# The first chunks' work and weight conversions in another order, and a decay table per chunk, in a retention and two-layer-pair kernel

## The chip, the cores and the metric

The kernel runs on one core of a Trainium2 chip. Its time is device microseconds (us) of one execution, from runs that repeat the same kernel. The core has TensorE (PE: matmuls; PEld: its weight loads), VectorE (DVE), ScalarE (ACT), GpSimd (POOL) and SyncE (SP), which issues the DMAs here. Each engine takes its instructions strictly in the order of its own queue, and engines wait for each other through semaphores.

## The reference

Retention over 4 sequences of 576 tokens with 8 heads of 64, and behind it two feed-forward pairs with 2304 tokens, 512 channels and 2048 hidden channels, all in fp32:

```python
# q, k, v: (4, 8, 576, 64)
scores = np.matmul(q, k.transpose(0, 1, 3, 2)) / np.sqrt(64)
gamma = 1.0 - 2.0 ** (-5.0 - np.arange(8))
Dmat = np.where(rel >= 0, gamma[:, None, None] ** rel, 0.0)   # rel = query position - key position
x = np.matmul(scores * Dmat, v)            # -> (2304, 512), tokens by channels
h = np.maximum(x @ w1_in, 0.0)
x = (h * h) @ w1_out                       # first pair
h = x @ w2_in
out = (h * np.clip(h + 3, 0, 6) / 6) @ w2_out   # second pair
```

## The kernel before

Tokens lie in 18 chunks of 128. The first pair runs over five blocks of tokens (512, 384, 512, 384, 512), and within a block over 16 steps f of 128 hidden channels each. In a step `h_part` makes the hidden rows (12 matmuls into a bank `h`), a relu, a product and a cast make `g`, and `a_part` adds 12 matmuls into four accumulators `acc`. On TensorE the order is h(0), h(1), acc(0), h(2), acc(1), h(3), acc(2) and so on.

fp32 numbers are carried as two fp32r parts, a high one (a cast) and a low one (what the cast left over), and each product takes three matmuls: high by high, high by low, low by high. The weights come as 64-bit words and are made fp32 on the core: `scale_w` (two instructions on ScalarE, lines 143 and 144), `narrow_w` (two on VectorE, 161 and 162), `cast_w` (the high part, ScalarE, 170) and `low_w` (the low part, GpSimd or VectorE, 177). Each step has two such halves of 512 columns: (f, 0) for `h_part`, (f, 1) for `a_part`. All of this is done while block 0 runs, a few steps ahead of use.

Before the first step, block 0's own input must be made: retention of chunks 0 to 3, the functions `first_...`. For a chunk c: `first_scores` (16 matmul records into `sc`), `first_mask` (VectorE, two instructions, `p`), `first_v` (v times a power of the decay, in place in `kv`), `first_values` (`p` by v into `o`), `first_read` (the state of the chunks before by q, added into the same `o`; chunk 0 has none), `first_states` (k by v, summed over the chunks into `total`, which is half of the PSUM tile `sums0`), `first_copy` (`total` into `states` in SBUF for the next chunk's read), `first_scale` (`o` times the decay table, `xf`), `first_x` (high part of x, ScalarE) and `first_low` (low part of x). Chunk 0's output is the other half of `sums0`. h(0) is done in two halves of 256 tokens: chunks 0 and 1, then chunks 2 and 3.

The order of every engine's queue is the order in which these calls are written; nothing is moved by a scheduler (`tc.manual_schedule()`). The DMAs of the start go through one queue in the written order too. `idle_matmuls` are matmuls on zeros whose output nobody reads.

Of the kernel before, what the change touches and what calls it, by code (L numbers as in the profile page):

```python
# [11 lines left out]
F32 = mybir.dt.float32  # L12
# [77 lines left out]
def retention_moe_kernel(ctx: ExitStack, tc, qk, kv, w1, w2, cst, out):  # L90
# [114 lines left out]
    def load_t(c):  # L205
        if c:
            tag = (None, f"w{NF - 5}_0", f"w{NF - 2}_0", f"w{NF - 2}_1")[c]
            t = whi.tile([P, 2, NPAIR, P], F32, tag=tag, name=f"q_{c}")
        else:
            t = apool.tile([P, 2, NPAIR, P], F32, tag="q", name=f"q_{c}")  # L210
        nc.sync.dma_start(t, qk[c].rearrange("p x (n t) -> p x n t", n=NPAIR))
        ch[c] = [t[:, 0], t[:, 1]]
# [33 lines left out]
    def first_v(c, eng):  # L246
        v3 = ch[c][3].rearrange("p (h d) -> p h d", h=H)
        eng.tensor_tensor(v3, v3, vds[c].unsqueeze(2).to_broadcast([P, H, D]), ALU.mult)  # L248
# [11 lines left out]
                r = slice(64 * e, 64 * e + 64)  # L260
                nc.tensor.matmul(sc[:, e, p, :], kt[r, p, :], q[r, p, :], start=True, stop=True)

    def first_mask(c):
        sc = points.pop(c)
        t = whi.tile([P, 2, NPAIR, P], F32, tag=f"w{NF - 4}_{1 - c % 2}", name=f"p_{c}")

        mask = causal.unsqueeze(1).to_broadcast([P, NPAIR, P])
        for i in range(2):
            a, b = (x[:, :, 2 * i : 2 * i + 2] for x in (t, sc))
            nc.vector.tensor_tensor(a, b, mask.rearrange("p (e n) t -> p e n t", e=2), ALU.mult)  # L270
        probs[c] = t

    def first_out(c):
        if c == 0:
            outs[c] = sums0[:, 1].rearrange("p (n t) -> p n t", n=NPAIR)
        else:
            outs[c] = ps_h.tile([P, NPAIR, P], F32, tag="h", name=f"o_{c}")

    def out_matmuls(c, first, last, stationary, moving):
        for p in range(NPAIR):  # L280
# [15 lines left out]
    def first_read(c, first=False, last=False):  # L296
# [4 lines left out]
            c, first, last, lambda p, e: s[:, p, 64 * e : 64 * e + 64], lambda p, e: q[:, p, :]  # L301
        )

    def first_scale(c):
        x = xf[c] = whi.tile(
            [P, NPAIR, P], F32, tag=(f"w{NF - 7}_{c % 2}", f"w{NF - 8}_{c % 2}")[c // 2], name=f"xf_{c}"
        )
        if c == 0:
            nc.vector.tensor_tensor(x, outs[c], qd3, ALU.mult)
            return  # L310
        for p in range(NPAIR):
            nc.vector.scalar_tensor_tensor(
                x[:, p], outs[c][:, p], gcs[c][:, p : p + 1], qd3[:, p], ALU.mult, ALU.mult
            )

    def first_x(c):
        x = xs[0, 0][:, :, :, c * P : (c + 1) * P]
# [295 lines left out]
    def h_part(ph, blk, f, between=lambda: None):  # L613
        nb = BLOCKS[blk][0]
        w = wts[ph, f, 0]
        x = xs[ph, blk]
        hp = ps_h.tile([P, 512], F32, tag="h", name=f"h_{ph}_{blk}_{f}")
        def order(last):
            return [(c, wi, xi) for wi, xi in ((0, 0), last[::-1], last) for c in range(NC)]

        parts = 2 if ph == blk == f == 0 else 1
        for i in range(parts):
            ts = slice(i * nb // parts, (i + 1) * nb // parts)
            for k, (c, wi, xi) in enumerate(order((1, 0) if blk == 0 and i == 0 else (0, 1))):
                nc.tensor.matmul(  # L625
                    hp[:, ts],
                    w[:, wi, c * P : (c + 1) * P],
                    x[:, xi, c, ts],
                    start=k == 0,
                    stop=k == 3 * NC - 1,  # L630
                )
        r = tmpp.tile([P, 512], F32, tag="tmp", name=f"r_{ph}_{blk}_{f}")
        r = r[:, :nb]
        nc.scalar.activation(r, hp[:, :nb], AF.Relu)  # L634
        between()
        nc.vector.tensor_tensor(r, r, hp[:, :nb], ALU.mult)  # L636
# [212 lines left out]
    def idle_matmuls(n):  # L849

        t = ps_h.tile([P, 512], F32, tag="h", name="unread")
        for _ in range(n):
            nc.tensor.matmul(t[:, :P], nought, nought, start=True, stop=True)

    idle_matmuls(6)
    for t in state:
        nc.vector.memset(t, 0.0)
    nc.vector.memset(con3, 3.0)
    load_t(0)
    nc.sync.dma_start(con0[:, :QD0], cst[:, :QD0])  # L860
    load_t(1)
    load_kv(0)
    load_kv(1)
    load_w(0, 0, (0,))
    load_t(2)
    nc.sync.dma_start(con0[:, QD0:], cst[:, QD0:DK0])
    load_kv(2)
    load_t(3)
    load_kv(3)
    load_w(0, 1, (0,))  # L870
    load_w(0, 0, (1,))
    load_w(0, 1, (1,))
    for f in range(2, 4):
        load_w(0, f)
    nc.sync.dma_start(con, cst[:, DK0:])
    new_x(0, 0)

    first_scores(0)
    first_mask(0)
    first_scores(1)  # L880
    idle_matmuls(3)
    first_v(0, nc.vector)
    first_mask(1)
    first_states(0)
    first_v(1, nc.gpsimd)
    first_values(0, first=True, last=True)
    first_copy(0, act=False)
    first_values(1, first=True)
    scale_w(0, 0, (0,))
    first_read(1, last=True)  # L890
    narrow_w(0, 0, (0,))
    first_states(1)
    first_scores(2)
    first_copy(1, act=True)
    first_scale(1)
    first_v(2, nc.gpsimd)
    first_read(2, first=True)
    first_scale(0)
    first_x(1)
    first_mask(2)  # L900
    first_low(1, nc.gpsimd)
    first_x(0)
    first_states(2)
    cast_w(0, 0, (0,))
    first_scores(3)
    first_copy(2, act=True)
    low_w(0, 0, (0,))
    first_v(3, nc.vector)
    first_values(2, last=True)
    first_mask(3)  # L910
    first_read(3, first=True)
    first_low(0, nc.gpsimd)
    scale_w(0, 1, (0,))
    first_scale(2)
    first_states(3)
    first_values(3, last=True)
    first_scale(3)
    first_x(3)
    narrow_w(0, 1, (0,))
    first_x(2)  # L920
    first_low(3, nc.gpsimd)
    first_low(2, nc.vector)
    scale_w(0, 0, (1,))
    cast_w(0, 1, (0,))
    low_w(0, 1, (0,))
    scale_w(0, 2, (0,))
# [45 lines left out]
    def first_between(f):  # L972
        if f == 0:
            scale_w(0, 1, (1,))
        if f + 2 < NF:
            cast_w(0, f + 2, (0,))
            low_w(0, f + 2, (0,))

    for i, (ph, blk, f) in enumerate(steps):
        if blk == 0:  # L980
            if 1 < f:
                low_w(0, f, (1,), nc.vector)
            if f:
                scale_ahead(f, True)
            if 0 < f < NF - 2:
                narrow_w(0, f + 2, (0,))
            if 0 < f < NF - 1:
                narrow_w(0, f + 1, (1,))

        late = i >= len(steps) - 2  # L990
        if not late:
            unit_work(i - NF + 2, 0)
        if i + 1 < len(steps):
            h_part(*steps[i + 1], lambda: first_between(f) if blk == 0 else None)
            if i == 0:
                narrow_w(0, 1, (1,))
            if blk == 0 and f + 1 < NF:
                cast_w(0, f + 1, (1,))
            if i == 0:
                g_low(*steps[1])  # L1000
                low_w(0, 1, (1,), nc.vector)
                scale_w(0, 3, (0,))
                first_sum()
                scale_w(0, 2, (1,))
            if blk == 0 and f:
                scale_ahead(f, False)
        if blk == 0:
# [298 lines left out]
```

## Time and profile before

| | us |
|---|---|
| median of 3 runs | 802.19 (802.16 to 804.36) |
| the profiled execution | 803.26 |
| its span, first to last instruction | 801.5 |
| TensorE busy | 795.2 (99%) |
| VectorE, ScalarE, GpSimd busy | 592.3, 399.6, 165.3 |

The profile is of one execution, whose own time stands beside its span; the rest of its time lies around the span. A page of it has the busy time of each engine, the chain of work that ended last, and the costliest lines. Here 96% of that chain is TensorE. The timeline of an engine lists its instructions by start time; consecutive instructions of one line are merged with their count. "[0.63 <-DMA q]" at the end of a row is idle time of the engine before that row and what ended it.

### The profile page before, as it was taken

The numbers are of one execution on the slowest core, as the hardware profiler recorded it, in microseconds if no ns is written. First come the engines' busy times: TensorE is split into PE (matmuls) and PEld (weight loads), VectorE is DVE, ScalarE is ACT, GpSimd is POOL, SyncE is SP. The second block draws the span as 40 slices with busy tenths as digits, with TensorE's granted clock in tenths as the row PEclk, the third lists the DMA queues.
The fourth block names the chain that finished last, engine by engine and source line by source line (L and its number), as shares of the span: only waits on it lengthen the run. The fifth ranks groups of instructions, "written<-read, shape, count | busy, mean of one in ns | idle before, by whom it ended". The sixth has DMA issues, their size and how long they took to land.

```text
span 801.5 us, 16527 instructions
## 1 busy us (share of the span) xinstructions
PE 795.2 (99%) x6390; PEld 741.2 (92%) x6390; DVE 592.3 (74%) x1091; ACT 399.6 (50%) x741; POOL 165.3 (21%) x154
## 2 busy tenths in 40 slices
PE   9999999999999999999999999999999999999998
PEld 8788889999888899998888899999999999999998
DVE  5988987878755587776557866987577987677864
ACT  3797744444443444444435533666234655244553
POOL 3312230211011011100000065600255500256200
PEclk9999999999999999999999999999999999999999
DMA  9966637777756487856448888888887989878884
GB/s 345 344 201 237 220 93 210 220 224 223 221 149 188 125 257 213 232 159 186 143 133 267 248 300 254 306 302 298 273 264 245 350 260 304 277 244 264 265 277 144
DMA packets 148062, 189.66 MB, mean 237 GB/s; under 512 B 22416, under 2 KB 101904, under 8 KB 147984
## 3 DMA queue, kind: packets, MB, share of 16 engines
q1 hardware_dynamic: 147984, 188.61, 74.0%
q8 instruction: 50, 0.82, 0.5%
q14 instruction: 28, 0.23, 0.1%
HBM read 149.78 MB, written 38.80 MB: 235 GB/s over the span
## 4 chain that ended last, share of the span: by engine, by line
PE 96%; DMA 2%; POOL 1%; issue 1%; DVE 0%; POOLq 0%
PE acc L662 25%; PE h L625 24%; PE z L1196 22%; PE z L1251 21%; PE at L498 2%; DMA kv<-kv_dram 1%; POOL x L322 1%; POOL w L177 1%; PE alone L498 0%; DMA q<-qk_dram 0%; PE sc L410 0%; PE o L461 0%; PE sc L421 0%; PE o L471 0%; POOL kv L248 0%
## 5 line engine op out<-in xcount | busy, mean ns | idle before, releaser
L662 PE MATMUL acc<-g,w 128*128 128x512 f32 (+1 forms) x960 | 213.1, 370 | 0.3 <-POOL w L177 0.3
L625 PE MATMUL h<-x,w 128*128 128x512 f32 (+2 forms) x972 | 210.9, 365 | 1.3 <-ACT x L318 0.6
L625 PEld LDWEIGHTS h<-x,w 128*128 128x128 f32 x972 | 175.9, 188 | 24.0 <-ACT x L318 0.8
L662 PEld LDWEIGHTS acc<-g,w 128*128 128x128 f32 x960 | 173.8, 188 | 24.5 <-POOL w L177 0.6
L1196 PE MATMUL z<-xop,ring 128*128 128x384 f32 x1008 | 175.3, 334 | 0.0
L1196 PEld LDWEIGHTS z<-xop,ring 128*128 128x128 f32 x1008 | 174.7, 188 | 0.1
L1251 PE MATMUL z<-ring,spl 128*128 128x256 f32 x1512 | 172.2, 276 | 0.0
L1251 PEld LDWEIGHTS z<-ring,spl 128*128 128x128 f32 x1512 | 172.1, 188 | 0.0
L1112 POOL TENSOR_TENSOR aop<-aop,aop 128x384 f32<-128x384 f32 x96 | 106.6, 1122 | 293.4 <-DVE aop L1109 289.7
L1134 DVE TENSOR_TENSOR spl<-aop,spl 128x384 fp32r<-128x384 f32 x168 | 99.1, 608 | 30.6 <-ACT spl L1130 27.0
L1130 ACT ACTIVATE spl<-aop 128x384 fp32r<-128x384 f32 x168 | 86.4, 524 | 54.4 <-PE z L1251 49.6
L634 ACT ACTIVATE r<-h 128x512 f32<-128x512 f32 (+1 forms) x80 | 44.3, 554 | 109.7 <-PE h L625 109.6
L1106 ACT ACTIVATE aop<-held,small 128x384 f32<-128x384 f32 x72 | 44.5, 619 | 108.3 <-DVE held L1072 107.8
L636 DVE TENSOR_TENSOR r<-r,h 128x512 f32<-128x512 f32 (+1 forms) x80 | 50.6, 632 | 53.3 <-ACT r L634 52.8
L1072 DVE TENSOR_TENSOR held<-z,held 128x384 f32<-128x384 f32 x120 | 66.5, 554 | 28.5 <-PE z L1196 26.4
L638 ACT ACTIVATE g<-r 128x512 fp32r<-128x512 f32 (+1 forms) x80 | 47.3, 591 | 65.8 <-DVE r L636 65.8
L644 DVE TENSOR_TENSOR g<-r,g 128x512 fp32r<-128x512 f32 (+1 forms) x80 | 53.1, 663 | 20.9 <-ACT g L638 18.6
L1109 DVE SCALAR_TENSOR_TENSOR aop<-aop,held 128x384 f32<-128x384 f32 x72 | 50.2, 698 | 17.8 <-ACT aop L1106 16.2
L395 POOL TENSOR_TENSOR qs<-qs,con 128x512 f32<-128x512 f32 x11 | 15.6, 1416 | 138.5 <-DMA qs<-qk_dram 138.5
L752 ACT ACTIVATE uhi<-seven 128x896 fp32r<-128x896 f32 x32 | 30.6, 956 | 24.3 <-DVE seven L742 14.1
L757 DVE TENSOR_TENSOR seven<-seven,uhi 128x896 fp32r<-128x896 f32 x32 | 34.9, 1091 | 7.6 <-ACT uhi L752 7.2
L177 POOL TENSOR_TENSOR w<-wt,w 128x512 fp32r<-128x512 f32 x17 | 23.1, 1359 | 63.6 <-ACT w L170 57.0
(109 smaller groups left out, 611.9 us busy)
## 6 DMA issues: line engine op xcount, KB each, us to landing
ring<-w_out_hl SPq DMA_DIRECT2D x84, 512.0 KB, 5.0
ring<-w_in_hl SPq DMA_DIRECT2D x72, 512.0 KB, 4.6
raw<-w_dram SPq DMA_DIRECT2D x32, 512.0 KB, 7.0
uraw<-w_dram SPq DMA_DIRECT2D x64, 256.0 KB, 3.4
q<-qk_dram SPq DMA_DIRECT2D x18, 512.0 KB, 5.2
w_in_hl<-uhi SPq DMA_DIRECT2D x16, 448.0 KB, 3.8
w_in_hl<-seven SPq DMA_DIRECT2D x16, 448.0 KB, 4.7
w_out_hl<-uhi SPq DMA_DIRECT2D x16, 448.0 KB, 3.2
```

The costliest lines, as they stand in the source:

```text
L625: nc.tensor.matmul(hp[:, ts], w[:, wi, c * P : (c + 1) * P], x[:, xi, c, ts], start=k == 0, stop=k == 3 * NC - 1,)
L636: nc.vector.tensor_tensor(r, r, hp[:, :nb], ALU.mult)
L638: nc.scalar.activation(g[:, 0, :nb], r, AF.Copy)
L644: nc.vector.tensor_tensor(g[:, 1, :nb], r, g[:, 0, :nb].bitcast(F32), ALU.subtract)
L662: nc.tensor.matmul(acc[d][:, :nb], wt, g[:, gi, :nb], start=first, stop=stop)
L1072: fn(*a)
L1109: stt(f32(q, j), f32(q, j), 6.0, h, ALU.min, ALU.mult)
L1112: nc.gpsimd.tensor_tensor(f32(o, j), f32(a, j), f32(b, j), op)
L1130: act(t[:, 0, :], f32(q, k), AF.Copy)
L1134: tt(t[:, 1, :], f32(q, k), t[:, 0, :].bitcast(F32), ALU.subtract)
L1196: nc.tensor.matmul(bank[q], w[:, wi, u * P : (u + 1) * P], x[:, u, xi, :], start=k == 0 and q not in (2, 4, 3), stop=k == 5, skip_group_ch ...
L1251: nc.tensor.matmul(o, sp[:, g, P * n : P * (n + 1)], w[:, k % 2, wi, :], start=k == 0 and m == 0 and n % 2 == 0 and q not in (2, 4, 3), st ...
```

## The change

Seven things are changed, all ahead of step 2 of block 0:

- k and v of chunk 0 are loaded third, the decay table (`con0`, second part) fourth, w(0,0) of step 0 after k, v of chunk 2; among the later weights some change places.
- The idle matmuls are 7 and 5 in place of 6 and 3, and the 5 stand behind the scores of chunk 0.
- `first_scores` of a chunk stands behind `first_states` of the chunk before, not a chunk ahead; `first_read` stands ahead of `first_values`.
- `first_mask` may be called in two halves; `first_low` of chunk 0 stands between the halves of chunk 1.
- A decay table `qds` is made per chunk (`first_decay`, two on VectorE, one on GpSimd), and `first_scale` is one `tensor_tensor` for each chunk in place of four `scalar_tensor_tensor`.
- Chunk 3's output, too, goes to the second half of `sums0`.
- In steps 0 and 1 of block 0 the work handed to `h_part` as `between` stands ahead of the relu; the relu of step 0 moves from ScalarE to VectorE; narrowing and cast of w(1,1) and the scaling of w(3,0) join step 0's `between`, which is the one handed to h(1).

```diff
-    def first_mask(c):
-        sc = points.pop(c)
-        t = whi.tile([P, 2, NPAIR, P], F32, tag=f"w{NF - 4}_{1 - c % 2}", name=f"p_{c}")
...
+    def first_mask(c, i):
+        sc = points[c]
+        if i == 0:
+            probs[c] = whi.tile(
+                [P, 2, NPAIR, P], F32, tag=f"w{NF - 4}_{1 - c % 2}", name=f"p_{c}"
+            )
...
     def first_out(c):
-        if c == 0:
+        if c % 3:
+            outs[c] = ps_h.tile([P, NPAIR, P], F32, tag="h", name=f"o_{c}")
+        else:
             outs[c] = sums0[:, 1].rearrange("p (n t) -> p n t", n=NPAIR)
...
+    qds = [qd3, qd2[0][:, 0], qd2[0][:, 1], qd2[1][:, 0]]
+
+    def first_decay(c, eng):
+        g = gcs[c].unsqueeze(2).to_broadcast([P, NPAIR, P])
+        eng.tensor_tensor(qds[c], qd3, g, ALU.mult)
+
     def first_scale(c):
...
-        for p in range(NPAIR):
-            nc.vector.scalar_tensor_tensor(
-                x[:, p], outs[c][:, p], gcs[c][:, p : p + 1], qd3[:, p], ALU.mult, ALU.mult
-            )
+        xf[c] = xf2[c // 2][:, c % 2]
+        nc.vector.tensor_tensor(xf[c], outs[c], qds[c], ALU.mult)
...
-        nc.scalar.activation(r, hp[:, :nb], AF.Relu)
-        between()
+        first = ph == blk == 0 and f < 2
+        if first:
+            between()
+        if ph == blk == f == 0:
+            nc.vector.tensor_scalar(r, hp[:, :nb], 0.0, None, ALU.max)
+        else:
+            nc.scalar.activation(r, hp[:, :nb], AF.Relu)
+        if not first:
+            between()
...
     load_t(0)
     nc.sync.dma_start(con0[:, :QD0], cst[:, :QD0])
+    load_kv(0)
+    nc.sync.dma_start(con0[:, QD0:], cst[:, QD0:DK0])
     load_t(1)
-    load_kv(0)
     load_kv(1)
+    load_t(2)
+    load_kv(2)
     load_w(0, 0, (0,))
...
     first_scores(0)
-    first_mask(0)
-    first_scores(1)
-    idle_matmuls(3)
-    first_v(0, nc.vector)
...
+    idle_matmuls(5)
+    first_v(0, nc.gpsimd)
+    first_mask(0, 0)
...
@@ first_between, called from h_part(0, 0, f + 1)
             cast_w(0, f + 2, (0,))
             low_w(0, f + 2, (0,))
+        if f == 0:
+            narrow_w(0, 1, (1,))
+            cast_w(0, 1, (1,))
+            scale_w(0, 3, (0,))
...
@@ the loop over steps
             h_part(*steps[i + 1], lambda: first_between(f) if blk == 0 else None)
-            if i == 0:
-                narrow_w(0, 1, (1,))
-            if blk == 0 and f + 1 < NF:
+            if blk == 0 and 0 < f < NF - 1:
                 cast_w(0, f + 1, (1,))
             if i == 0:
                 g_low(*steps[1])
                 low_w(0, 1, (1,), nc.vector)
-                scale_w(0, 3, (0,))
```

ScalarE's queue from the cast of w(0,1) on, in the kernel before. In the names the step and the half follow (`w_2_0` is step 2's first half), `r` is the relu's output, `raw` a weight being scaled, and the last number only counts tiles:

```order
L170 ACTIVATE w_0_1_390<-wt_0_1_387 128x512
L638 ACTIVATE g_0_0_394<-r_0_0_385 128x512
L634 ACTIVATE r_0_1_425<-h_0_1_412 128x512
L143 ACTIVATE raw_1_1_150<-raw_1_1_150 128x512
L144 ACTIVATE raw_1_1_150<-raw_1_1_150 128x512
L170 ACTIVATE w_2_0_429<-wt_2_0_396 128x512
L638 ACTIVATE g_0_1_433<-r_0_1_425 128x512
L170 ACTIVATE w_1_1_438<-wt_1_1_435 128x512
L143 ACTIVATE raw_3_0_156<-raw_3_0_156 128x512
L144 ACTIVATE raw_3_0_156<-raw_3_0_156 128x512
```

The same place of ScalarE's queue in the changed kernel:

```order
L170 ACTIVATE w_0_1_385<-wt_0_1_382 128x512
L649 ACTIVATE g_0_0_390<-r_0_0_381 128x512
L143 ACTIVATE raw_1_1_157<-raw_1_1_157 128x512
L144 ACTIVATE raw_1_1_157<-raw_1_1_157 128x512
L170 ACTIVATE w_2_0_424<-wt_2_0_392 128x512
L170 ACTIVATE w_1_1_430<-wt_1_1_427 128x512
L143 ACTIVATE raw_3_0_159<-raw_3_0_159 128x512
L144 ACTIVATE raw_3_0_159<-raw_3_0_159 128x512
L644 ACTIVATE r_0_1_421<-h_0_1_408 128x512
L649 ACTIVATE g_0_1_436<-r_0_1_421 128x512
```

The relu of step 1 and the cast of g(1) moved from the third and seventh place to the last two, behind the cast of w(1,1) and the scaling of w(3,0).

VectorE's queue at the same steps, before, from the product of step 0 to the low part of w(1,1) (`wt` is a narrowed weight):

```order
L636 TENSOR_TENSOR r_0_0_385<-r_0_0_385,h_0_0_360 128x512
L161 TENSOR_SCALAR wt_2_0_396<-raw_2_0_152 128x512
L162 ISA wt_2_0_396<-raw_2_0_152,wt_2_0_396 128x1024
L644 TENSOR_TENSOR g_0_0_394<-r_0_0_385,g_0_0_394 128x512
L636 TENSOR_TENSOR r_0_1_425<-r_0_1_425,h_0_1_412 128x512
L161 TENSOR_SCALAR wt_1_1_435<-raw_1_1_150 128x512
L162 ISA wt_1_1_435<-raw_1_1_150,wt_1_1_435 128x1024
L644 TENSOR_TENSOR g_0_1_433<-r_0_1_425,g_0_1_433 128x512
L177 TENSOR_TENSOR w_1_1_438<-wt_1_1_435,w_1_1_438 128x512
```

And in the changed kernel:

```order
L642 TENSOR_SCALAR r_0_0_381<-h_0_0_356 128x512
L647 TENSOR_TENSOR r_0_0_381<-r_0_0_381,h_0_0_356 128x512
L161 TENSOR_SCALAR wt_2_0_392<-raw_2_0_155 128x512
L162 ISA wt_2_0_392<-raw_2_0_155,wt_2_0_392 128x1024
L655 TENSOR_TENSOR g_0_0_390<-r_0_0_381,g_0_0_390 128x512
L161 TENSOR_SCALAR wt_1_1_427<-raw_1_1_157 128x512
L162 ISA wt_1_1_427<-raw_1_1_157,wt_1_1_427 128x1024
L647 TENSOR_TENSOR r_0_1_421<-r_0_1_421,h_0_1_408 128x512
L655 TENSOR_TENSOR g_0_1_436<-r_0_1_421,g_0_1_436 128x512
L177 TENSOR_TENSOR w_1_1_430<-wt_1_1_427,w_1_1_430 128x512
```

The relu of step 0 came to VectorE, and the product of step 1 moved behind the narrowing of w(1,1).

VectorE's queue in the first chunks, before: the scaling of chunks 1 and 0 (lines 312 and 309), and the masks of chunks 2 and 3 (line 270):

```order
L344 COPY states<-sums_103 64x4x64 x2
L161 TENSOR_SCALAR wt_0_0_229<-raw_0_0_135 128x512
L162 ISA wt_0_0_229<-raw_0_0_135,wt_0_0_229 128x1024
L312 SCALAR_TENSOR_TENSOR xf_251<-o_210,con_99 128x128 x4
L309 TENSOR_TENSOR xf_266<-sums_103,con_99 128x512
L270 TENSOR_TENSOR p_269<-sc_240,con_99 128x2x256 x2
L248 TENSOR_TENSOR kv_144<-kv_144,con_99 128x512
L270 TENSOR_TENSOR p_305<-sc_284,con_99 128x2x256 x2
```

And in the changed kernel, from the two tables to the mask of chunk 3 (line 318 scales chunks 0, 1 and 2, line 271 masks chunks 1 to 3, line 326 is the low part of chunk 0):

```order
L314 TENSOR_TENSOR qd_106<-con_99 128x512 x2
L318 TENSOR_TENSOR xf_104<-sums_103,con_99 128x512
L271 TENSOR_TENSOR p_228<-sc_207,con_99 128x2x256
L326 TENSOR_TENSOR x_0_166<-xf_104,x_0_166 128x4x128
L271 TENSOR_TENSOR p_228<-sc_207,con_99 128x2x256
L318 TENSOR_TENSOR xf_104<-o_219,qd_106 128x512
L271 TENSOR_TENSOR p_262<-sc_251,con_99 128x2x256 x2
L318 TENSOR_TENSOR xf_105<-o_264,qd_106 128x512
L161 TENSOR_SCALAR wt_0_0_305<-raw_0_0_145 128x512
L162 ISA wt_0_0_305<-raw_0_0_145,wt_0_0_305 128x1024
L271 TENSOR_TENSOR p_318<-sc_296,con_99 128x2x256 x2
```

The narrowing of w(0,0) moved from the chunk 1 scaling to just ahead of the mask of chunk 3, and the low part of chunk 0 stands between the two mask instructions of chunk 1.

## Rows read from the trace of the kernel before

**Rows 1.** Waits of TensorE, whole run: total us, times, longest (first and last of five)

```profile
PE unread L853 <- POOL nought L847: 1.0, 1, 1.0
...
PE acc L662 <- POOL w L177: 0.3, 1, 0.3
```

**Rows 2.** Timeline of TensorE: start us, us, line, operation, count, idle before

```profile
4.56 3.78 PE L261 MATMUL sc<-q 64*128 64x128 f32 x32 [0.63 <-DMA q<-qk_dram]
8.27 1.65 PE L853 MATMUL unread<-nought 128*128 128x128 f32 x6
...
14.05 1.16 PE L261 MATMUL sc<-q 64*128 64x128 f32 x16
15.15 1.09 PE L282 MATMUL o<-q,states 128*64 128x128 f32 x16
16.07 0.63 PE L328 MATMUL sums<-kv 128*64 128x64 f32 x16
...
21.14 1.67 PE L625 MATMUL h<-x,w 128*128 128x256 f32 x12
...
25.22 3.46 PE L625 MATMUL h<-x,w 128*128 128x256 f32 x16 [0.56 <-DVE x L322]
...
29.26 2.83 PE L662 MATMUL acc<-g,w 128*128 128x512 f32 x11 [0.32 <-POOL w L177]
31.92 2.88 PE L625 MATMUL h<-x,w 128*128 128x512 f32 x12
34.64 2.89 PE L662 MATMUL acc<-g,w 128*128 128x512 f32 x12
...
41.29 3.02 PE L662 MATMUL acc<-g,w 128*128 128x512 f32 x12
```

**Rows 3.** Timeline of ScalarE, the first 46 us

```profile
14.16 0.78 ACT L342 ACTIVATE states<-sums 64x256 f32<-64x256 f32 x2 [2.12 <-PE sums L328]
...
27.75 0.64 ACT L638 ACTIVATE g<-r 128x512 fp32r<-128x512 f32 x1
28.72 0.60 ACT L634 ACTIVATE r<-h 128x512 f32<-128x512 f32 x1 [0.33 <-PE h L625]
29.21 0.67 ACT L143 ACTIVATE raw<-raw 128x512 f32<-128x512 f32 x1
...
33.02 0.64 ACT L170 ACTIVATE w<-wt 128x512 fp32r<-128x512 f32 x1 [1.41 <-DVE wt L162]
```

**Rows 4.** Timeline of VectorE, the first 46 us

```profile
6.68 1.29 DVE L270 TENSOR_TENSOR p<-sc,con 128x512 f32<-128x512 f32 x2 [4.73 <-PE sc L261]
8.11 0.69 DVE L248 TENSOR_TENSOR kv<-kv,con 128x512 f32<-128x512 f32 x1
...
13.12 0.69 DVE L162 CUSTOM_DVE_ANT_0 wt<-raw,wt 128x1024 uint16<-128x1024 uint16 x1
13.83 1.13 DVE L312 SCALAR_TENSOR_TENSOR xf<-o,con 128x128 f32<-128x128 f32 x4
14.98 0.69 DVE L309 TENSOR_TENSOR xf<-sums,con 128x512 f32<-128x512 f32 x1
...
17.47 1.29 DVE L248 TENSOR_TENSOR kv<-kv,con 128x512 f32<-128x512 f32 x1 [0.61 <-DMA kv<-kv_dram]
...
31.42 1.57 DVE L162 CUSTOM_DVE_ANT_0 wt<-raw,wt 128x1024 uint16<-128x1024 uint16 x1
...
33.69 0.69 DVE L177 TENSOR_TENSOR w<-wt,w 128x512 fp32r<-128x512 f32 x1
...
39.84 0.68 DVE L177 TENSOR_TENSOR w<-wt,w 128x512 fp32r<-128x512 f32 x1
```

**Rows 5.** Timeline of GpSimd, the first 46 us

```profile
9.49 1.04 POOL L248 TENSOR_TENSOR kv<-kv,con 128x512 f32<-128x512 f32 x1 [8.56 <-DMA kv<-kv_dram]
...
27.86 1.34 POOL L177 TENSOR_TENSOR w<-wt,w 128x512 fp32r<-128x512 f32 x1 [1.29 <-ACT w L170]
31.03 1.41 POOL L177 TENSOR_TENSOR w<-wt,w 128x512 fp32r<-128x512 f32 x1 [1.83 <-DMA qs<-qk_dram]
```

More of the change, by code (lines that the diff above doesn't have):

```diff
@@ L261, in first_scores @@
                 nc.tensor.matmul(sc[:, e, p, :], kt[r, p, :], q[r, p, :], start=True, stop=True)
-    def first_mask(c):
-        sc = points.pop(c)
-        t = whi.tile([P, 2, NPAIR, P], F32, tag=f"w{NF - 4}_{1 - c % 2}", name=f"p_{c}")
+    def first_mask(c, i):
[4 more added lines that the diff above has]
+            )
         mask = causal.unsqueeze(1).to_broadcast([P, NPAIR, P])
[L268 to L271, printed above, removed]
+        a, b = (x[:, :, 2 * i : 2 * i + 2] for x in (probs[c], sc))
+        nc.vector.tensor_tensor(a, b, mask.rearrange("p (e n) t -> p e n t", e=2), ALU.mult)
     def first_out(c):
-        if c == 0:
+        if c % 3:
+            outs[c] = ps_h.tile([P, NPAIR, P], F32, tag="h", name=f"o_{c}")
+        else:
             outs[c] = sums0[:, 1].rearrange("p (n t) -> p n t", n=NPAIR)
-        else:
-            outs[c] = ps_h.tile([P, NPAIR, P], F32, tag="h", name=f"o_{c}")
     def out_matmuls(c, first, last, stationary, moving):
@@ L302, in first_read @@
         )
-    def first_scale(c):
-        x = xf[c] = whi.tile(
-            [P, NPAIR, P], F32, tag=(f"w{NF - 7}_{c % 2}", f"w{NF - 8}_{c % 2}")[c // 2], name=f"xf_{c}"
-        )
-        if c == 0:
-            nc.vector.tensor_tensor(x, outs[c], qd3, ALU.mult)
-            return
-        for p in range(NPAIR):
-            nc.vector.scalar_tensor_tensor(
-                x[:, p], outs[c][:, p], gcs[c][:, p : p + 1], qd3[:, p], ALU.mult, ALU.mult
-            )
+    xf2 = [
+        whi.tile([P, 2, NPAIR, P], F32, tag=f"w{NF - 7}_{i}", name=f"xf_{i}") for i in range(2)
+    ]
+    qd2 = [
+        whi.tile([P, 2, NPAIR, P], F32, tag=f"w{NF - 8}_{i}", name=f"qd_{i}") for i in range(2)
+    ]
+    qds = [qd3, qd2[0][:, 0], qd2[0][:, 1], qd2[1][:, 0]]
+    def first_decay(c, eng):
+        g = gcs[c].unsqueeze(2).to_broadcast([P, NPAIR, P])
+        eng.tensor_tensor(qds[c], qd3, g, ALU.mult)
+    def first_scale(c):
+        xf[c] = xf2[c // 2][:, c % 2]
+        nc.vector.tensor_tensor(xf[c], outs[c], qds[c], ALU.mult)
     def first_x(c):
@@ L853, in idle_matmuls @@
             nc.tensor.matmul(t[:, :P], nought, nought, start=True, stop=True)
-    idle_matmuls(6)
+    idle_matmuls(7)
     for t in state:
@@ L860, in retention_moe_kernel @@
     nc.sync.dma_start(con0[:, :QD0], cst[:, :QD0])
+    load_kv(0)
+    nc.sync.dma_start(con0[:, QD0:], cst[:, QD0:DK0])
     load_t(1)
-    load_kv(0)
     load_kv(1)
+    load_t(2)
+    load_kv(2)
     load_w(0, 0, (0,))
-    load_t(2)
-    nc.sync.dma_start(con0[:, QD0:], cst[:, QD0:DK0])
-    load_kv(2)
     load_t(3)
@@ L871, in retention_moe_kernel @@
     load_w(0, 0, (1,))
+    load_w(0, 2, (0,))
     load_w(0, 1, (1,))
-    for f in range(2, 4):
-        load_w(0, f)
+    load_w(0, 3, (0,))
+    load_w(0, 2, (1,))
+    load_w(0, 3, (1,))
     nc.sync.dma_start(con, cst[:, DK0:])
@@ L878, in retention_moe_kernel @@
     first_scores(0)
-    first_mask(0)
+    idle_matmuls(5)
+    first_v(0, nc.gpsimd)
+    first_mask(0, 0)
+    first_mask(0, 1)
+    first_values(0, first=True, last=True)
+    first_decay(2, nc.vector)
+    first_decay(1, nc.vector)
+    first_states(0)
+    first_decay(3, nc.gpsimd)
+    first_copy(0, act=True)
     first_scores(1)
-    idle_matmuls(3)
-    first_v(0, nc.vector)
-    first_mask(1)
-    first_states(0)
+    first_scale(0)
+    first_x(0)
     first_v(1, nc.gpsimd)
[L886 to L891, printed above, removed]
+    first_read(1, first=True)
+    first_mask(1, 0)
+    first_low(0, nc.vector)
+    first_mask(1, 1)
+    first_values(1, last=True)
     first_states(1)
-    first_scores(2)
     first_copy(1, act=True)
     first_scale(1)
+    first_scores(2)
     first_v(2, nc.gpsimd)
+    first_x(1)
+    first_mask(2, 0)
     first_read(2, first=True)
-    first_scale(0)
-    first_x(1)
-    first_mask(2)
     first_low(1, nc.gpsimd)
-    first_x(0)
+    first_mask(2, 1)
+    first_values(2, last=True)
+    scale_w(0, 0, (0,))
     first_states(2)
+    first_scale(2)
+    first_copy(2, act=True)
+    first_scores(3)
+    narrow_w(0, 0, (0,))
+    first_x(2)
+    first_read(3, first=True)
+    first_v(3, nc.gpsimd)
+    first_mask(3, 0)
     cast_w(0, 0, (0,))
-    first_scores(3)
-    first_copy(2, act=True)
+    first_mask(3, 1)
     low_w(0, 0, (0,))
[L908 to L912, printed above, removed]
+    first_values(3, last=True)
+    first_states(3)
+    first_low(2, nc.vector)
     scale_w(0, 1, (0,))
-    first_scale(2)
-    first_states(3)
-    first_values(3, last=True)
     first_scale(3)
     first_x(3)
+    scale_w(0, 0, (1,))
     narrow_w(0, 1, (0,))
[L920 to L923, printed above, removed]
+    first_low(3, nc.vector)
     cast_w(0, 1, (0,))
```

## The prediction, made before the changed kernel ran

> **What bounds the kernel now.** I read the waits of TensorE over the whole run first, then the timelines of the engines over the first 46 us. TensorE has five waits that the profile names in 801.5 us, the longest 1.0 us and the last of the list 0.3 us [rows 1], and all lie ahead of 29.26 us, where the last one ends [rows 2]. From the acc row at 29.26 on its work is one gapless chain, 2.72 us for twelve matmuls of 512 columns (31.92 to 34.64) [rows 2]. Below, h(f) are the twelve matmuls of step f that make the hidden rows and acc(f) the twelve that use them; w(f,0) are step f's first weights, w(f,1) its second. Nothing after 34.64 can get shorter by this change, and any hold that TensorE gets there is added in full. So the question is when acc(1) can run: before, its second matmul stands at 34.64 + 0.23 = 34.87 us.
>
> The slack there is small. acc(1)'s second matmul needs the low part of w(1,1), which VectorE makes at 33.69 to 34.38, 0.5 us ahead [rows 4]. Its first matmul needs g(1) from ScalarE, which took relu r(1) at 28.72, as soon as h(1) was done, and only then scaled w(1,1) at 29.21 [rows 3]. The conversions of weights on ScalarE, VectorE and GpSimd are thus nearly as long as TensorE's own chain.
>
> **The change, part by part.** The differences end before step 2: behind it all five engines have the same instructions in the same order.
>
> Loads: k and v of chunk 0 come third, one load of 512 KB earlier than before, when their product started at 8.11 [rows 4]; they are no later now. The loads ahead of k, v of chunk 3 are the same set, so that one still lands at 17.45 (the row of 17.47) [rows 4]. GpSimd's product takes 1.04 [rows 5], so values(3) can't start before 18.5, and h(0) not before 18.5 + 0.9 + 0.6 = 20.0.
>
> First chunks on TensorE. Full-level prices: scores 1.10 (14.05 to 15.15), state read 0.92 (15.15 to 16.07), values the same, states about 0.6 [rows 2]. Up to about 8.3 the matmuls are slower: 32 records of scores take 3.78 us, where 16 take 1.16 later. By these rows the clock stands at the lower of its two levels (1.2 and 2.4 GHz) there. The masks of chunk 0 still end at 6.68 + 1.29 = 7.97 [rows 4]. scores(0), sixteen records from 4.56, are through at about 6.4, and the five idle matmuls, ten records at some 0.22 us a piece (six took 1.65 with the tail of the last), cover the time up to 8.5, or up to 8.1 if the level rises in them. In that case values(0) run from 8.1 to 9.0; at the slow pace they end near 10.2. Both stay as cases; I take the first, because the pause of 0.63 us ahead of the first scores [rows 2] gets shorter by the seventh idle matmul, two records or about 0.4 us. The Trainium skill's "TensorE: Matmul & The Clock Gate" (Part 1: The HAM clock gate) says that the default is the throttled state and that sustained activity releases it; by that rule the denser start brings the rise forward and the total is the 805.0 below; if it stays where it was, the 806.4 of the late case.
>
> From 9.0 the new order is a chain: states 0.58, then three rounds of scores, read, values, states, each 1.10 + 0.89 + 0.89 + 0.58 = 3.46; 9.0 + 0.58 + 10.38 = 19.96 without a hold. Holds: the first scaling reads the PSUM tile that ScalarE's copy of the state reads and stands behind that copy, as before, where it started at 14.98, right behind the copy of 14.16 + 0.78 [rows 3, 4]. So copy to 10.5, scale to 11.2, x on ScalarE to 11.9, low part on VectorE 11.96 to 12.6 and only then the second half of mask 1, to 13.2: TensorE could have gone on at about 12.0, hold 1.25. In chunk 3 the narrowing of w(0,0) stands ahead of the mask (1.13, and it meets GpSimd's product): hold 0.6. h(0) starts at 19.96 + 1.85 = 21.8 to 21.95, against 21.14 before [rows 2].
>
> Scaling with tables: twelve instructions (three of four, 1.13 per four) become three of 0.66 plus two table products on VectorE and one on GpSimd: about 3.4 - 3.2 us on VectorE, nothing, and the tables lie in its idle time before 10 us. Values products leave VectorE (0.7 and 1.3), but two low parts come to it; nothing net. The fourth output's bank and the state read ahead of values remove no wait that the list of TensorE's waits names; I set them at nothing beside the order worked out above.
>
> h(0): twelve matmuls 1.5 us to 23.4. The second half needs x of chunk 3: values(3) end 21.6, then VectorE's low part of chunk 2, behind GpSimd's low part of w(0,0), until 22.2; scale 22.9; cast 23.55. Narrowing w(1,0) 1.15, low part of chunk 3 to 24.6, the last four matmuls from 24.65: h(0) ends at 25.35. Before, these four started at 25.22 [rows 2], so 0.6 us are won by here. h(1): 25.4 to 28.15. acc(0) needs w(0,1)'s low part from GpSimd at 28.5 (before 29.26 [rows 2]): 0.7 us won. h(2) to 33.9.
>
> Then the term that decides. r(0) moves to VectorE: narrowing ends 26.0, relu 26.7, square 27.35, g(0) on ScalarE 27.4 to 28.05 (before 27.75 [rows 3]). Now ScalarE's order is: scale w(1,1) (two, 28.0 to 29.3), cast w(2,0) (its narrowing waits for GpSimd at 28.5 and ends 29.65: cast to 30.3), cast w(1,1), scale w(3,0), and only then relu r(1). Narrowing w(1,1) starts at 30.2; its second half meets GpSimd's low part of w(2,0), as before, when it took 1.57 instead of the 0.69 of 13.12 (31.42, GpSimd 31.03 + 1.41) [rows 4, 5], so it ends at 32.45. From there, with handovers of 0.03 to 0.06 (31.42 + 1.57 to 33.02; 27.86 + 1.34 to 29.26 [rows 2 to 5]): cast w(1,1) 33.1, scale w(3,0) 2 x 0.57 to 34.3, relu 34.95, square 0.66 to 35.65, g(1) 36.35, low part of g(1) 37.05, low part of w(1,1) 37.65. Behind the relu, VectorE holds all of this in its queue, and TensorE waits for it: acc(1) could have started at 33.9, its first matmul goes at 36.4, its second at 37.7.
>
> Sum: 37.7 - 34.87 = +2.8 us. Behind it nothing grows: before, step 2's low weights ended at 40.52, 1.0 us ahead of acc(2)'s second matmul at 41.29 + 0.23 [rows 2, 4]. And nothing comes back, since TensorE's chain has no gap that could give it back. In the profiled execution that is 801.5 + 2.8 = 804.3 of span, and with the 1.8 us around it 806.1 (803.26 before). The median of the runs shown, 802.19, lies 1.1 below the profiled run, so I forecast 802.19 + 2.8 = 805.0.
>
> **The rivals.**
> *Late clock.* The early matmuls stay at the slow pace until about 10.3, as before. Then values(0) end 1.2 later, the first scaling meets GpSimd's product of chunk 2 in the low part, and h(0) ends at 26.9; everything behind is 1.55 later, less 0.1 where a hold shrinks: +4.2, 806.4. For it: before showed that pace up to 9.9. Against: the pause is shorter.
>
> *Port order.* VectorE's narrowing of w(1,1) gets ahead of GpSimd's low part of w(2,0). Then it isn't held 1.1 us: +1.7, 803.9. For it: both become ready within 0.3 us. Against: the same pair met in the same way before. The Trainium skill's "SBUF — State Buffer" (Who interferes with whom) has the pair of ports as a lock that the first comer keeps for a whole instruction, and the row of 1.57 agrees; so the start order alone would settle this case.
>
> *The first chunks reach the floor of the loads.* If scale, x and low part of chunk 0 don't hold the mask and the narrowing doesn't hold mask 3, h(0) starts at 20.0 and ends at 23.5, 1.85 earlier than in my sum; then g(0), and the chain behind it, too: +0.9, 803.1. For it: the load of chunk 3 allows it. Against: scale, cast, low part and mask are four serial steps on two engines.
>
> *Not slower: the relu is hidden.* TensorE works 5.44 us on acc(0) and h(2) behind h(1). If relu r(1), square, g(1) and the low parts are through in that time, acc(1) starts when TensorE is ready for it, 33.9 in place of 34.64: -0.75, 801.4. For it: before, relu r(1) to the end of the low part of w(1,1) took 28.72 to 34.38, 5.7 us [rows 3, 4], about as much. Against: there r(1) ran beside the scaling and narrowing of w(1,1), and now it stands behind them and behind w(3,0); in my sum the stretch from the end of h(1) at 28.15 is 9.5 us long. It decides from the point where that stretch is under 5.8 us. Only with the floor as well, -2.6, would the change be measurably faster.
>
> **How the numbers follow.** A difference under 0.3% (2.4 us) can't be told from no change. Forecast (+2.8, between +2.0 and +3.6) 0.45; late clock 0.20; port order 0.15; floor 0.10; hidden relu 0.10. Slower: most of the forecast (0.33) and the late clock: 0.53. Faster: the hidden relu together with the floor, and what I don't see: 0.07. Same: the rest, 0.40. The range runs from a little under the floor to a little over the late clock: 802.0 to 806.8.
>
> **What would show it.** In the new profile TensorE should wait some 3 us at acc, around 34 to 37.7, for ScalarE's g and VectorE's w, a wait that was not there; relu of h(1) should start 5 us or more after h(1) ends, behind the scaling of w(3,0); h(0) should start near 22 and end near 25.4. The forecast is wrong if that wait is under 1 us, or if h(0) ends before 24.

## The result, and the profile after

The changed kernel takes 807.92 us (median of 6 runs, 805.42 to 808.47); the kernel before, in 6 runs beside them, 802.50 (802.16 to 804.77). The ratio is 1.0055, with a 95% interval of 1.0036 to 1.0073: slower, by 5.4 us between the medians. The forecast was 805.0 with a range up to 806.8, and the measured median lies above that range. The direction came true; the step forecast, 2.8 us, is half of the 5.4. One execution timed for this document, of the last experiment's kernel, took 1129.67 us with a mean granted clock of 0.656, and its ratio leaves that one out.

The profiled execution of the changed kernel is the fastest of its six: 805.42 us with a span of 803.6, 2.2 above the profiled execution of before (803.26, 801.5). TensorE's waits over the whole run, six of seven in the form of [rows 1]:

```profile
PE acc L673 <- ACT g L649: 1.9, 1, 1.9
PE unread L864 <- POOL nought L858: 1.0, 1, 1.0
PE acc L673 <- DVE w L177: 0.8, 1, 0.8
PE o L282 <- DVE p L271: 0.7, 1, 0.7
PE sums L282 <- POOL kv L248: 0.7, 1, 0.7
PE sums L282 <- issue: 0.4, 1, 0.4
...
```

The two at acc are new, 1.9 + 0.8 = 2.7 us. TensorE's timeline, with the columns of [rows 2], shows where they stand:

```profile
4.60 1.16 PE L261 MATMUL sc<-q 64*128 64x128 f32 x16 [0.25 <-DMA q<-qk_dram]
...
7.75 1.09 PE L282 MATMUL sums<-p,kv 128*64 128x128 f32 x16 [0.68 <-POOL kv L248]
...
12.91 0.66 PE L282 MATMUL o<-p,kv 128*64 128x128 f32 x8 [0.69 <-DVE p L271]
...
21.74 6.31 PE L629 MATMUL h<-x,w 128*128 128x256 f32 x36
27.89 3.06 PE L673 MATMUL acc<-g,w 128*128 128x512 f32 x12
30.78 2.88 PE L629 MATMUL h<-x,w 128*128 128x512 f32 x12
35.55 0.50 PE L673 MATMUL acc<-g,w 128*128 128x512 f32 x1 [1.89 <-ACT g L649]
36.88 2.79 PE L673 MATMUL acc<-g,w 128*128 128x512 f32 x11 [0.83 <-DVE w L177]
39.56 3.04 PE L629 MATMUL h<-x,w 128*128 128x512 f32 x12
```

acc(0) starts at 27.89, where it was held until 29.26 before, h(2) at 30.78 instead of 31.92 [rows 2]. TensorE is thus 1.1 us ahead when it comes to acc(1). There it stands still, and acc(1)'s second matmul goes at 36.88, 2.0 later than before (34.64 + 0.23). The lead is lost, and two microseconds more.

ScalarE shows why (g(0), cast of w(2,0), cast of w(1,1), second instruction of the scaling of w(3,0), relu of h(1), g(1)):

```profile
26.91 0.64 ACT L649 ACTIVATE g<-r 128x512 fp32r<-128x512 f32 x1 [0.32 <-DVE r L647]
...
29.13 0.63 ACT L170 ACTIVATE w<-wt 128x512 fp32r<-128x512 f32 x1 [0.46 <-DVE wt L162]
31.77 0.63 ACT L170 ACTIVATE w<-wt 128x512 fp32r<-128x512 f32 x1 [2.01 <-DVE wt L162]
...
32.85 0.64 ACT L144 ACTIVATE raw<-raw 128x512 int32<-128x512 uint32 x1
33.52 0.60 ACT L644 ACTIVATE r<-h 128x512 f32<-128x512 f32 x1
34.87 0.63 ACT L649 ACTIVATE g<-r 128x512 fp32r<-128x512 f32 x1 [0.75 <-DVE r L647]
```

h(1) ends near 27.9, when acc(0) begins, but its relu starts at 33.52, 5.6 us later. Before, ScalarE stood waiting for h(1) and took it at 28.72 [rows 3]. For 2.01 us ScalarE even stands idle in front of the cast of w(1,1), with the relu's input ready and the relu three places behind in its queue. VectorE in the same stretch (the second half of the narrowing of w(1,1), the square and g(1)'s low part, and w(1,1)'s low part), and the GpSimd row that stands beside the first:

```profile
30.17 1.56 DVE L162 CUSTOM_DVE_ANT_0 wt<-raw,wt 128x1024 uint16<-128x1024 uint16 x1
34.15 0.69 DVE L647 TENSOR_TENSOR r<-r,h 128x512 f32<-128x512 f32 x1 [2.42 <-ACT r L644]
35.53 0.69 DVE L655 TENSOR_TENSOR g<-r,g 128x512 fp32r<-128x512 f32 x1 [0.70 <-ACT g L649]
36.14 0.69 DVE L177 TENSOR_TENSOR w<-wt,w 128x512 fp32r<-128x512 f32 x1
```

```profile
29.84 1.35 POOL L177 TENSOR_TENSOR w<-wt,w 128x512 fp32r<-128x512 f32 x1 [1.86 <-DMA qs<-qk_dram]
```

VectorE's low part of w(1,1) had its inputs since 32.4, but stands behind the square and g(1)'s low part in its queue, so it ends at 36.83, and TensorE goes on at 36.88.

That explains the 2.2 us between the two profiled executions. The medians are 5.4 apart. The other five executions have a mean granted clock of 0.996 to 0.998 over the span, the profiled one 1.000, and they take 806.84 to 808.47. The open question was what happens in them.

### The profile page after: what moved, and what is told of

Same layout as the page of the kernel before. It is cut to its first block, busy times and chain, and to the rows that moved or that the text cites. A ratio compares the mean times of both kernels' runs of the same rounds, so it can differ in the third digit from the quotient of the medians.

```text
span 803.6 us, 16536 instructions
## 1 busy us (share of the span) xinstructions
PE 794.7 (99%) x6396; PEld 739.5 (92%) x6396; DVE 591.6 (74%) x1083; ACT 399.7 (50%) x742; POOL 165.2 (21%) x155
## 4 chain that ended last, share of the span: by engine, by line
PE 96%; DVE 2%; DMA 1%; ACT 1%; issue 1%; POOL 0%; SPq 0%; DVEq 0%; POOLq 0%
PE acc L673 25%; PE h L629 24%; PE z L1217 22%; PE z L1272 21%; PE at L502 2%; DMA kv<-kv_dram 1%; PE alone L502 1%; DVE wt L161 0%; DVE wt L162 0%; PE o L282 0%; DVE x L326 0%; PE sc L414 0%; PE o L465 0%; PE sc L425 0%; DVE p L271 0%
```

## The experiments

Two theories went into the first experiments. A: the order of steps 0 and 1 is the whole cause; TensorE waits at acc(1), and in most executions its granted clock falls behind that wait. B: the first chunks have part in it, by a clock that rises late in some executions or by loads that land later (the expectations call the loads' part C). Each kernel ran beside the kernel before on the same chip. That one took 803.04 us beside the first four (21 runs) and 802.98 beside the last two (15 runs). The ratios are recorded with their intervals and can differ by a few ten-thousandths from the quotient of two medians.

**The changed kernel once more.** No edit.

> The changed kernel unchanged. Its five other runs took 806.8 to 808.5 us with a mean granted clock of 0.996 to 0.998, the profiled one 805.4 with 1.000. Theory A (the wait of 2.7 us at acc(1) lets the clock fall to its lower level for a stretch behind it, in most runs): 807 to 808.5 us again, and where the mean clock is under 1.000 the profile shows half clock in one stretch shortly behind 33 us, with matmuls of 512 columns there at about 0.43 us each. Rival B (the clock only rises late in the first chunks): the missing clock lies ahead of 15 us, none behind 33. Rival C (later or earlier landings of the loads): the clock shows nothing, kv of chunk 3 lands over 1 us later than 17.3.

Measured: 806.91 us (5 runs, 806.33 to 807.95), ratio 1.0052 (1.0040 to 1.0065). This time the profiled execution is one of the longer kind, 806.91 with a span of 805.1. Two of its stretches follow (columns: window, its length, busy us and count of PE, PEld, DVE, ACT, POOL, granted clock, DMA share, GB/s):

```profile
36.60:40.10 3.50, 2.88 (x7) 2.30 (x8) 3.29 (x7) 1.47 (x3) 0.18 (x1) 0.51 0.67 268
40.10:44.00 3.90, 3.90 (x20) 2.94 (x18) 3.73 (x7) 2.96 (x6) 1.33 (x1) 1.00 0.02 6
```

And its TensorE:

```profile
22.07 6.31 PE L629 MATMUL h<-x,w 128*128 128x256 f32 x36
...
35.89 0.50 PE L673 MATMUL acc<-g,w 128*128 128x512 f32 x1 [1.88 <-ACT g L649]
37.22 4.12 PE L673 MATMUL acc<-g,w 128*128 128x512 f32 x11 [0.83 <-DVE w L177]
41.18 2.88 PE L629 MATMUL h<-x,w 128*128 128x512 f32 x12
```

The waits are the same, 1.88 and 0.83. But in the stretch in which TensorE comes out of them the granted clock is 0.51, the lower of the two levels (1.2 of 2.4 GHz), and the eleven matmuls of acc(1) take 4.12 us instead of 2.79. The same stretch of the execution shown above has full clock:

```profile
36.60:40.10 3.50, 3.22 (x13) 2.47 (x14) 3.25 (x8) 1.13 (x3) 0.52 (x1) 1.00 0.63 253
```

h(3) starts at 41.18 here and at 39.56 there, 1.62 later: 0.33 of it was there at h(0) already (22.07 against 21.74), and 1.3 is the clock. The spans differ by 1.5. Theory A's second half is seen. Not seen is what B and C asked for: the scores in the first chunks run slower here (1.83 us for sixteen records, against 1.16), but k and v of chunk 3 are taken up 0.3 later than there (17.61, against 17.27), not over 1 us, and all the start makes together is the 0.33. The Trainium skill's "TensorE: Matmul & The Clock Gate" (Part 1: The HAM clock gate) has the throttled state as the one that an idle TensorE goes back to. That agrees in kind with the 0.51; the 1.00 of the other execution shows that this wait brings it in some executions only.

**h(2) done twice.** TensorE has no long wait then, though the other engines work as before. Step 2's hidden rows are computed a second time, which leaves the output as it is.

```diff
-        for i in range(parts):
+        for i in range(parts) if (blk, f) != (0, 2) else (0, 0):
```

> As the changed kernel, but the twelve matmuls of h(2) are done twice into the same bank, the second time anew from the start, so that TensorE works through most of the wait at acc(1) (30.8 to 36.2 in place of 30.8 to 33.5); acc(1)'s second matmul still waits for the low part of w(1,1) at 36.9. By waits alone this costs 0 to 0.4 us. A: the clock stays at 1.000 in all runs and the median falls to 805.2 to 806.0. B and C: 807.9 to 808.3, with the same clock as the changed kernel.

Measured: 806.06 us (5 runs, 805.69 to 806.99), ratio 1.0042 (1.0028 to 1.0056), just above the number expected.

```profile
31.25 5.62 PE L629 MATMUL h<-x,w 128*128 128x512 f32 x24
36.71 0.39 PE L673 MATMUL acc<-g,w 128*128 128x512 f32 x1
37.37 2.79 PE L673 MATMUL acc<-g,w 128*128 128x512 f32 x11 [0.27 <-DVE w L177]
```

Twelve more matmuls, and it is 0.85 us faster than the changed kernel beside it, in the median; the two ranges of five runs overlap (805.69 to 806.99, and 806.33 to 807.95). acc(1)'s second matmul is no earlier (37.37 against 37.22), but its eleven take 2.79 again. The clocks are the clearer sign: the means of its five runs are 0.999 to 1.000, as in all 36 runs of the kernel before, where nine of the eleven runs of the changed kernel have 0.998 or 0.996. What filled the wait kept the clock up. 3.0 us are left over the kernel before, and 2.5 of them stand at acc(1): 37.37 against 34.64 + 0.23 [rows 2].

**The relu of h(1) ahead of the conversions.** Of the step order one thing is taken back: h(1)'s relu stands ahead of `between` again. Its square, g(1) and the low parts stay behind it.

```diff
-        if first:
+        if first and f == 0:
             between()
...
-        if not first:
+        if not first or f == 1:
             between()
```

> As the changed kernel, but in step 1 the relu of h(1) stands ahead of the conversions in ScalarE's queue again; the product on VectorE and the cast g(1) stay behind them. By the rows of the changed kernel: relu at 28.1, scale w(1,1) to 29.75, narrowing to 32.25 (it meets GpSimd), cast 32.9, scale w(3,0) to 34.0, g(1) 34.6, low parts to 35.95, so acc(1)'s second matmul at 36.0 in place of 36.9. The wait at acc(1) stays, over 2 us. A: 1 us less than the changed kernel, 806 to 807.5, and the clock still falls in most runs. If the relu's place alone were the cause: 802 to 803.

Measured: 803.33 us (11 runs, 803.04 to 804.73), ratio 1.0004 (0.9995 to 1.0013). The slowdown is gone, and what was expected missed it by 3 us. The profile says where. TensorE:

```profile
22.17 6.31 PE L629 MATMUL h<-x,w 128*128 128x256 f32 x36
...
33.93 0.39 PE L673 MATMUL acc<-g,w 128*128 128x512 f32 x1
34.95 2.79 PE L673 MATMUL acc<-g,w 128*128 128x512 f32 x11 [0.63 <-DVE w L177]
```

ScalarE (relu, cast of w(2,0), cast of w(1,1), g(1)):

```profile
28.52 0.60 ACT L644 ACTIVATE r<-h 128x512 f32<-128x512 f32 x1 [0.55 <-PE h L629]
...
30.14 0.64 ACT L170 ACTIVATE w<-wt 128x512 fp32r<-128x512 f32 x1
31.32 0.63 ACT L170 ACTIVATE w<-wt 128x512 fp32r<-128x512 f32 x1 [0.55 <-DVE wt L162]
...
32.95 0.62 ACT L649 ACTIVATE g<-r 128x512 fp32r<-128x512 f32 x1
```

VectorE's narrowing of w(1,1), second half, and GpSimd's low part of w(2,0):

```profile
30.60 0.69 DVE L162 CUSTOM_DVE_ANT_0 wt<-raw,wt 128x1024 uint16<-128x1024 uint16 x1
```

```profile
30.85 1.60 POOL L177 TENSOR_TENSOR w<-wt,w 128x512 fp32r<-128x512 f32 x1 [2.44 <-DMA qs<-qk_dram]
```

Counted from the start of h(0), g(1) is cast at 32.95 - 22.17 = 10.78 us, in the changed kernel at 34.87 - 21.74 = 13.13: 2.35 earlier. The relu that now runs ahead made the cast of w(2,0) later, so GpSimd's low part of w(2,0) starts at 30.85, behind VectorE's narrowing and not 0.33 ahead of it, and the narrowing takes 0.69 instead of 1.56. That is 0.87 of the 2.35. The other 1.5 are relu and square, 0.60 + 0.69 and their handovers, which no longer stand between the scaling of w(3,0) and g(1). The wait at acc(1) is 0.63, and no execution of the eleven has a mean clock under 0.999. What I had expected differs first at the narrowing: held by GpSimd, it was to end at 32.25, and it ends at 31.29, which is 1.4 earlier when both are counted from h(0). acc(1)'s second matmul comes 1.5 earlier than the 36.0 expected, counted in the same way. With the wait so short, the fall of the clock that I had expected stays out too.

**The first chunks of the changed kernel, steps 0 and 1 in the old order.** The loads, the first chunks and step 0's relu on VectorE stay as changed. `between` stands behind the relu of h(1) again, and narrowing and cast of w(1,1) and the scaling of w(3,0) go back to the loop over steps.

```diff
-        first = ph == blk == 0 and f < 2
+        first = ph == blk == f == 0
...
-        if f == 0:
-            narrow_w(0, 1, (1,))
-            cast_w(0, 1, (1,))
-            scale_w(0, 3, (0,))
...
+            if i == 0:
+                narrow_w(0, 1, (1,))
-            if blk == 0 and 0 < f < NF - 1:
+            if blk == 0 and f + 1 < NF:
                 cast_w(0, f + 1, (1,))
...
+                scale_w(0, 3, (0,))
```

> The first chunks, loads and the relu of step 0 as in the changed kernel, but steps 1 and 2 in the order of the kernel before: relu, scale w(1,1), cast w(2,0), g(1), cast w(1,1), scale w(3,0) on ScalarE, and the product ahead of the narrowing on VectorE. By the rows: relu of h(1) 28.05, g(1) 30.95, low part of w(1,1) 33.7, acc(1)'s second matmul at 33.75 with almost no wait, 1.1 us earlier than before's 34.87. A: no wait, so no fall of the clock: 1.1 under the kernel before, 801.4 us, at most 1 us more where the first rise comes late. B: the first chunks are the slow part, so this stays at 804 or more.

Measured: 802.72 us (11 runs, 802.49 to 803.80), ratio 1.0000 (0.9992 to 1.0009). All the slowdown goes with the order of the steps, and the new first chunks cost or bring nothing that can be measured. The 801.4 expected did not come. In the profiled execution TensorE has no wait at acc(1), but it waited 1.67 for the product of chunk 0's v (0.68 in the changed kernel), and h(0) starts 1.1 later than there, which is the whole gain expected:

```profile
8.50 1.09 PE L282 MATMUL sums<-p,kv 128*64 128x128 f32 x16 [1.67 <-POOL kv L248]
...
22.83 6.33 PE L629 MATMUL h<-x,w 128*128 128x256 f32 x36
29.00 3.05 PE L673 MATMUL acc<-g,w 128*128 128x512 f32 x12
...
34.63 3.07 PE L673 MATMUL acc<-g,w 128*128 128x512 f32 x12
```

**The first chunks of before, steps 0 and 1 in the changed order.** The counterpart: the last experiment's lines turned round, put into the kernel before, with step 0's relu on VectorE.

> Steps 0 and 1 in the changed order (relu of step 0 on VectorE, relu of step 1 behind the conversions) behind the kernel before's own first chunks and loads. If the order of the steps alone makes the slowdown: h(1) ends about 1.0 to 1.4 us later than in the changed kernel, so the chain of relu, product, g(1) and low part ends that much later, acc(1)'s second matmul at about 38.1 us where TensorE is ready at 34.9: a wait of 3.2 us, and behind it a granted clock of about 0.5 in some stretch near 38 to 41 us that costs another 1 to 1.5: 3.2 to 4.7 over the kernel before, 806.0 to 807.7 where it has 803.0. If the first chunks' order takes part in it (late clock, later loads): the wait is under 1 us and the time within 1 us of the kernel before.

Measured: 807.27 us (5 runs, 805.77 to 808.77), ratio 1.0056 (1.0043 to 1.0070): the slowdown of the changed kernel in full, with none of its first chunks.

```profile
28.58 3.03 PE L669 MATMUL acc<-g,w 128*128 128x512 f32 x12 [0.48 <-ACT g L645]
...
36.13 0.50 PE L669 MATMUL acc<-g,w 128*128 128x512 f32 x1 [1.80 <-ACT g L645]
37.46 2.77 PE L669 MATMUL acc<-g,w 128*128 128x512 f32 x11 [0.82 <-DVE w L177]
```

The wait is 1.80 + 0.82 = 2.6 us, and acc(1)'s second matmul goes at 37.46, not at 38.1, since all of it came 0.7 earlier in this execution (acc(0) at 28.58, against 29.26 [rows 2]). The profiled execution (806.03) shows full clock behind the wait; it and one of 805.77 have a mean clock of 1.000, the other three 0.996 to 0.999 and 807.27 to 808.77. With this, B is out: neither the new chunks nor the new loads are needed.

**The changed first chunks without three of their holds.** This is built on the kernel of 802.72: both mask halves of chunk 1 ahead of the low part of chunk 0, the product of chunk 0's v on VectorE behind the masks, and the narrowing of w(0,0) one place earlier.

```diff
-    first_v(0, nc.gpsimd)
     first_mask(0, 0)
     first_mask(0, 1)
+    first_v(0, nc.vector)
...
-    first_low(0, nc.vector)
     first_mask(1, 1)
+    first_low(0, nc.vector)
...
+    narrow_w(0, 0, (0,))
     first_scale(2)
     first_copy(2, act=True)
     first_scores(3)
-    narrow_w(0, 0, (0,))
```

> The changed first chunks with steps 1 and 2 in the order of the kernel before, and three holds of the first chunks taken away: both halves of the mask of chunk 1 ahead of the low part of chunk 0 (0.7 us), the narrowing of w(0,0) ahead of the scaling of chunk 2 in place of the mask of chunk 3 (0.5 to 0.7), the product of chunk 0's v on VectorE (0.69) in place of GpSimd (1.04). If TensorE's chain alone counts: h(0) starts at 20.3 to 20.9 us, acc(1) at 32.7 to 33.5 without a wait, 1.2 to 1.8 under the kernel before: 801.2 to 801.8 where it has 803.0. If the conversions of weights are the limit: VectorE's low part of w(1,1) still ends near 34.8, TensorE waits at acc(0) or acc(1) for what it won, and the time is within 0.5 of the kernel before.

Measured: 801.85 us (median of 11 runs, ten of them 801.08 to 802.67), ratio 0.9986 (0.9977 to 0.9995). That is 1.1 us under the kernel before and just above the 801.2 to 801.8 expected; the interval only just leaves out 1, and the difference is smaller than the 0.3% that the prediction counts as measurable. Over their kernels before, this one and the changed one stand at 0.9986 and 1.0055, 0.7% apart.

```profile
9.10 1.09 PE L282 MATMUL sums<-p,kv 128*64 128x128 f32 x16 [1.30 <-DVE kv L248]
...
22.06 6.29 PE L629 MATMUL h<-x,w 128*128 128x256 f32 x36
...
33.84 3.05 PE L673 MATMUL acc<-g,w 128*128 128x512 f32 x12
```

The profiled execution is one of the slower ones (802.67), with a wait of 1.30 for chunk 0's v, so its h(0) starts at 22.06, later than expected. Still acc(1) starts at 33.84 without a wait, 0.8 ahead of before. VectorE's low part of w(1,1) came forward with it, so the conversions are not a floor yet:

```profile
33.35 0.69 DVE L177 TENSOR_TENSOR w<-wt,w 128x512 fp32r<-128x512 f32 x1
```

## Why the prediction missed, and what of it held

*The place and the mechanism held.* A wait of "some 3 us at acc, around 34 to 37.7" was foretold, and 2.7 us between 33.6 and 36.9 came. The relu starts 5.6 us after the end of h(1); foretold was 5 or more. The queues' order gave both, and the experiments with one half of the change each (802.72 and 807.27) show that this order is sufficient and necessary.

*The front.* h(0) starts at 21.74; the sum had 21.8 to 21.95. This is partly luck: the hold at mask 1 is 0.69 where I had 1.25, the one in chunk 3 0.38 where I had 0.6 (the profile names nothing that it waited for), and a wait of 0.68 for chunk 0's v, which I had at nothing, fills the gap. "They are no later now" was wrong in its use: k and v of chunk 0 do land earlier (4.9 us after their issue at 1.6; before, 6.0 after 2.1), but in the new order nothing but the idle matmuls covers GpSimd's product of v, which starts at 6.66 and takes 1.04. The hold of the second half of h(0) until 24.65 did not come, and acc(0) starts at 27.89 instead of 28.15.

*The sum at acc(1).* Second matmul 36.88, predicted 37.7: 0.8 less. The narrowing of w(1,1) starts 0.6 earlier (29.61 to 31.73 with its 1.56, against 30.2 to 32.45), and the rest follows step for step. The port order was as assumed: GpSimd first, 1.56. For the profiled execution the step gives 801.5 + 2.0 = 803.5, and its span is 803.6.

*The step that failed* is "Behind it nothing grows", and with it the way from one execution to the median. For the wait I charged the time that TensorE stands still. It also costs the clock behind it: 0.51 from 36.6 to 40.1 in one execution, 1.3 us. The eleven runs of the changed kernel show it as a family. Two have a mean granted clock of 1.000 and take 805.42 and 806.33, six have 0.998 and take 806.75 to 807.95, three have 0.996 and take 807.90 to 808.47. A mean of 0.998 over 805 us is some 1.6 us of full clock lost, part of it inside the wait, where it costs nothing; 0.996 is some 3.2. The step that took the profiled execution's +2.8 over to the median, 802.19 + 2.8, assumed that both kernels spread alike around it. They don't: before, the profiled execution stands above its median, after, it is the fastest: 5.4 is 2.2 between the two, 2.5 from the profiled execution of the changed kernel up to its median, and 0.8 down to the median before (802.50). Of the 2.5 the traced fall shows 1.3. How large the clock's share is depends on how many of a few runs fell: with the wait filled the kernel stands 3.0 above the kernel before, close to the 2.8 forecast, and with the wait 3.9 and 4.3 in the two experiments that have it, 5.4 in the six runs of the result, three of which have 0.996.

*The rivals.* The late clock, which I feared in the first chunks, did not come: the scores of chunk 0 took 1.16 us for sixteen records in one execution and 1.83 in the other, where 32 took 3.78 [rows 2]; the values of chunk 0 took 1.09 in both. That the early pace is the clock's lower level was read from the durations alone: the granted clock in the profile is 1.00 there too (4.5 to 8.3 us of the kernel before). A clock that falls after the wait was not among the cases. Port order: not in the changed kernel, but it decides 0.87 us when the relu goes first, where I had 1.1. The floor of the loads was not reached, with 0.69 + 0.68 + 0.38 us of waits left between the idle matmuls and h(0). The hidden relu is refuted by the relu's row at 33.52.

*What stays open.* Why the same wait lets the clock fall in one execution and not in the other: the two profiled ones show waits equal to 0.01 us. The same section of the Trainium skill has the gate judge activity in a rhythm of its own that a kernel's start doesn't reset; by that rule one wait can go either way, but no run here shows that rhythm. The executions with 0.996 have no trace, so whether their clock falls longer or twice can't be told. Nor is it shown why executions at full clock differ: those of the kernel before take 802.16 to 804.77. The start is one candidate, since the mean clock does not show a slow pace there, and since chunk 0's v is taken up between 6.66 and 7.41 in the traces of the new first chunks that have its product on GpSimd.

## What to carry to other kernels

Where TensorE works without gaps at full clock, charge a new wait like this one twice: its length, and slower work behind it in some executions, here 1.3 us in the one traced for a wait of 2.7. Where the trace shows a wait of 0.63 there, no run of eleven had such a fall. Don't take the median from one profiled execution; look at the mean clock of every run before you say that nothing comes behind. In a strict queue, put what the bottleneck waits for ahead of what is only due later: a relu of 0.6 us, put behind a cast that waits 2 us, cost more than the new first chunks could give.

## What the runs showed of the hardware that was not expected

Twelve more matmuls made the kernel 0.85 us faster in the median than the same kernel with a wait in their place (806.06 against 806.91, with ranges that overlap); its granted clock stayed up in all five runs. And a row of VectorE's narrowing takes 0.69 or 1.56 us by whether GpSimd's instruction of 1.35 to 1.60 us starts 0.25 after it or 0.33 before it; a moved instruction on ScalarE, which is neither of the two engines, turned the order round.
